# A new hand-written order of work units for attention with a maxout feed-forward layer, with fewer zero matmuls at the head and other engines for some copies

## The chip, the cores and the metric

One core of one Trainium2 chip. A core has a matmul engine (PE; its weight loads are shown apart as PEld), a vector engine (DVE), an activation engine (ACT), a third elementwise engine (POOL) and a queue engine that starts transfers (SP). The metric is the time of one execution in device microseconds, the median of several runs.

## The reference

Attention over 4 batches, 8 heads, 768 positions and 64 channels per head. A query sees the last 96 keys and the first 8 ("global") keys; distance gives a bias that falls with a slope per head. The heads are joined to 3072 rows of 512 columns, which pass through a layer with three weight matrices, of whose products the maximum is taken, and an output matrix.

```
scores = scale * q @ k.T - slope[h] * dist      # kept where global or 0 <= i - j < 96
a = exp(scores - max); a = a / (sum(a) + 1e-9)
x = (a @ v) as 3072 x 512
h = max(max(x @ w1, x @ w2), x @ w3)            # 3072 x 768
out = h @ w_out                                  # 3072 x 512
```

## The kernel before

The 3072 rows are cut into 24 tiles T of 128 rows, six to a batch. Because of the window a tile needs only its own keys and values, those of the tile before it, and the 8 global ones. The tiles are joined in seven chunks of 4, 2, 2, 4, 4, 4, 4 tiles for the feed-forward part, so its matmuls have 512 or (chunks 1 and 2) 256 columns.

The whole order of work is written by hand: SCHEDULE (lines 25 to 57) is a list of units, each a letter, numbers, and often a last number that chooses an engine. The loop at line 475 issues them one after another. Nothing is reordered later: each engine, and the SP queue too, works its own instructions off in the order of the list and waits where an operand or a buffer isn't ready. The units:

- `l n.s`, `L T`, `v T`, `w g.j`, `o i` load q and k (l in larger parts for tiles 0 to 11, L for a single tile), v, the three weights and w_out, all on the SP queue.
- `c n.s.e`, `C T.0.e`, `C T.1.e`, `W g.j.e`, `Q i.e` cast q/k, v (`C T.1`), weights and w_out to bf16. The engine e is 0 for ACT, 1 for DVE, 2 for POOL.
- `x n.s.how` and `X T.how` transpose q and k: on PE into PSUM with a copy out by ACT (0, 2), DVE (1, 3) or, in halves, both (x with 4, X with 3); `X T.4` is a transposing transfer on SP.
- `S T.g.how` makes the scores of four heads on PE (16 small matmuls for both g together; with how 1 also two matmuls that add the bias) and their exponential on ACT (line 288). `M T.g` multiplies by the mask on DVE (line 307) where how was 0.
- `G T.e` and `V T.e` put the global keys and values into the first 8 places of a tile that is no longer needed as it was.
- `A T.slot` is the product with v on PE (lines 322 and 325), then on DVE a reciprocal and a product (lines 331 and 332) into xb.
- `T T.how` transposes xb: on PE with a copy by ACT (0) or DVE (1), or (4) as a transfer on SP.
- `F c.f.j` is four matmuls of chunk c (line 361): for j=0 ACT casts the result out of PSUM (366), for j=1 and j=2 DVE takes the maximum (368, 370). `O c.t.e` is the output product, six matmuls (376), with a copy by engine e (382) and the store. `E` is the last chunk's output.
- `B h.e` and `K h` build bias and mask tables. `D i.n` issues n matmuls of zeros with 512 columns (lines 432 to 436); its first number isn't used.

Scores and products with v share two PSUM slots, sp0 and sp1, one buffer each: `A T.0` takes sp0. F, O and some transposes share three buffers called h; the other transposes share one called tp. There are six buffers for exponentials, four for h01 and three for xT.

The first feed-forward matmul, F0.0.0, needs all of tiles 0 to 3, so it comes behind A0 to A3 and T0 to T3. It is preceded on PE by the scores of tile 4.

Of the kernel before, what the change touches and what calls it, by code (L numbers as in the profile page):

```python
# [22 lines left out]


SCHEDULE = """
    K0 K1 K2 l1.0 B0.2 B1.1 B2.1 K3 K4 K5 K6 B3.0 B4.1 l1.1 D1.4 B5.0 c0.0.2 B6.0 c0.1.1 D0.4 v0 l2.0
    x0.0.3 K7 x0.1.4 c1.0.1 v1 l2.1 B7.0 S0.0.1 S0.1.1 G0.2 S1.0.0 M0.0 M0.1 c1.1.1 c2.0.2 x1.0.2 x1.1.0
    C0.1.1 A0.0 S1.1.1 G1.1 v2 v3 S2.0.1 S2.1.0 G2.1 T0.1 M1.0 M1.1 c2.1.1 S3.0.1 M2.0 M2.1 C1.1.2
    C2.1.1 M3.0 S3.1.1 M3.1 A1.0 V1.2 x2.0.2 C3.1.2 w0.0 A2.1 x2.1.0 V2.2 A3.0 T1.0 w0.1 G3.2 W0.0.2
    T2.1 T3.1 S4.0.0 S4.1.0 w0.2 F0.0.0 F0.1.0 W0.2.1 G4.2 w1.0 W0.1.2 F0.0.1 F0.1.1 F0.0.2 F0.1.2  # L30
    S5.0.0 S5.1.0 V3.2 M4.0 W1.0.2 F0.2.0 M4.1 M5.0 F0.3.0 v4 w1.1 W2.1.0 W2.0.2 F0.4.0 F0.5.0 W1.1.1
    C4.1.2 w1.2 W1.2.2 M5.1 v5 A4.1 l3.0 l3.2 l3.1 C5.1.0 V4.2 F0.2.1 c3.0.0 F0.3.1 F0.4.1 T4.0 F0.5.1
    A5.1 F0.2.2 c3.2.0 F0.3.2 W2.2.2 F0.4.2 x3.0.2 T5.1 F0.5.2 x3.2.1 F1.0.0 F1.1.0 l3.3 l4.0 F1.0.1
    F1.1.1 c3.1.2 c3.3.2 F1.0.2 x3.1.4 F1.2.0 F1.2.1 x3.3.1 F1.3.0 c4.0.0 o2 F1.1.2 o1 Q1.1 F1.4.0 Q2.2
    S6.0.0 S6.1.0 G6.2 M6.0 o0 F1.5.0 F1.2.2 F1.3.1 S7.0.0 S7.1.0 v6 l4.1 v7 F1.4.1 G7.0 M6.1 v8 F1.3.2
    x4.0.0 L12 v9 M7.0 L13 Q0.2 O0.0.1 S8.0.0 M7.1 c4.1.1 S8.1.0 C6.1.2 F1.5.1 O0.1.0 A6.0 x4.1.2 C7.1.2
    A7.1 V7.1 G8.2 F1.4.2 F1.5.2 S9.0.0 S9.1.0 G9.2 v10 T6.1 M8.0 O0.2.1 T7.1 C8.1.0 v11 S10.0.0 S10.1.0
    G10.0 M8.1 M9.0 M9.1 O0.3.0 A8.0 F2.0.0 V8.2 F2.1.0 F2.0.1 F2.1.1 C9.1.2 C12.0.2 C13.0.2 C10.1.0
    F2.0.2 F2.1.2 A9.1 M10.0 M10.1 V9.1 X12.0 F2.2.0 F2.3.0 S11.0.0 S11.1.0 T8.4 M11.0 X13.4 F2.4.0 L14
    O1.0.1 L15 T9.0 F2.2.1 A10.1 F2.5.0 V10.2 F2.3.1 F2.4.1 S12.0.0 S12.1.0 M11.1 M12.0 F2.2.2 F2.3.2  # L40
    F2.4.2 v12 C11.1.2 A11.0 C14.0.0 X14.4 T10.0 v13 v14 M12.1 v15 F2.5.1 C12.1.2 F2.5.2 O1.1.1 G12.1
    S13.0.0 S13.1.0 G13.1 T11.1 O2.0.0 F3.0.0 M13.0 F3.0.1 M13.1 F3.1.0 F3.2.0 A12.1 C15.0.0 F3.0.2
    S14.0.0 X15.4 S14.1.0 T12.4 C13.1.1 F3.1.1 F3.2.1 v16 L16 L17 G14.0 L18 A13.0 F3.1.2 F3.2.2 F3.3.0
    M14.0 T13.1 F3.3.1 F3.3.2 V13.2 S15.0.0 S15.1.0 G15.0 F3.4.0 C14.1.2 F3.5.0 M14.1 M15.0 M15.1 A14.0
    V14.2 F3.4.1 F3.5.1 T14.4 F3.4.2 C15.1.2 F3.5.2 A15.0 L19 v17 C16.0.2 C17.0.2 X16.0 O2.1.0 X17.4
    T15.1 S16.0.0 v18 v19 S16.1.0 C18.0.2 G16.0 M16.0 O3.0.1 O3.1.1 F4.0.0 V15.2 F4.1.0 F4.2.0 F4.3.0
    C16.1.2 M16.1 A16.1 C19.0.2 X18.3 X19.4 F4.0.1 F4.0.2 S17.0.0 S17.1.0 M17.0 F4.1.1 C17.1.1 F4.1.2
    S18.0.0 S18.1.0 C18.1.1 F4.2.1 F4.3.1 T16.4 M17.1 F4.2.2 F4.3.2 G18.0 S19.0.0 M18.0 M18.1 L20 M19.0
    C19.1.1 L21 S19.1.0 F4.4.0 F4.5.0 G19.2 V16.2 C20.0.0 L22 A17.0 F4.4.1 M19.1 F4.5.1 F4.4.2 F4.5.2
    X20.4 T17.4 A18.1 T18.4 A19.0 T19.4 O3.2.0 O3.3.0 C21.0.1 C22.0.0 O4.0.0 S20.0.0 S20.1.0 M20.0 X21.4  # L50
    v20 G20.0 V19.1 M20.1 O4.1.0 F5.0.0 F5.1.0 F5.2.0 F5.0.1 F5.1.1 S21.0.0 S21.1.0 F5.0.2 F5.3.0 F5.1.2
    C20.1.2 A20.1 G21.1 X22.4 V20.2 F5.4.0 L23 F5.5.0 S22.0.0 S22.1.0 v21 v22 v23 C21.1.2 C22.1.2
    C23.0.0 X23.4 M21.0 M21.1 M22.0 F5.2.1 F5.3.1 F5.4.1 F5.5.1 F5.2.2 C23.1.1 F5.3.2 A21.1 F5.4.2
    F5.5.2 G22.2 S23.0.0 T20.4 S23.1.0 T21.4 O4.2.0 M22.1 M23.0 M23.1 V21.2 A22.0 O4.3.0 V22.2 A23.1
    T22.4 T23.4 O5.0.0 O5.1.0 O5.2.0 O5.3.0 F6.0.0 F6.1.0 F6.2.0 F6.0.1 F6.1.1 F6.0.2 F6.2.1 F6.1.2
    F6.3.0 F6.2.2 F6.4.0 F6.5.0 F6.3.1 F6.4.1 F6.3.2 F6.4.2 F6.5.1 F6.5.2 E
"""


# [450 lines left out]
```

## Time and profile before

| what | value |
|---|---|
| median of 4 runs | 181.33 us (180.77 to 181.77) |
| profiled execution, its own time | 182.91 us |
| its span, first to last instruction | 181.1 us |
| PE busy | 169.4 us (94%) |
| DVE / ACT / POOL busy | 121.0 / 103.3 / 39.0 us |
| DMA read and written | 25.17 MB and 6.29 MB |

The difference of 1.8 us between the profiled time and its span lies around the instructions. PE is by far the busiest, but its share is a mean over two unlike stages: a head of some 24 us, in which the first inputs arrive, and the long rest. The rows are read stage by stage for that reason. One caution on PE: the ends of matmuls are modelled, so each row shows a duration longer than the spacing of successive matmuls; the spacing is what counts.

### The profile page before, as it was taken

The page shows a single profiled execution, that of the slowest core. Times are in us where ns is not written, and L with a number is a line of the kernel's source. Part 1 is how long each engine was busy: PE and PEld are TensorE (multiplying, and loading weights), DVE is VectorE, ACT ScalarE, POOL GpSimd, SP SyncE. Part 2 cuts the span into 40 slices and gives each one's busy share as a digit, 9 for nine tenths or more (in the row PEclk, how much of TensorE's full clock was granted, in tenths as well). Part 3 has the DMA queues.
Part 4 walks back from the last instruction along what each step waited for, and adds up shares of the span by engine and source line. Part 5 has one row for each costly group of instructions (what it writes and reads, how often), then busy time and mean ns, then how long its engine had stood idle before and what let it go on. Part 6 is the DMA issues. An engine that isn't in the chain of part 4 may idle for free.

```text
span 181.1 us, 3964 instructions
## 1 busy us (share of the span) xinstructions
PE 169.4 (94%) x1535; PEld 96.4 (53%) x1556; DVE 121.0 (67%) x236; ACT 103.3 (57%) x158; POOL 39.0 (22%) x66
## 2 busy tenths in 40 slices
PE   7688689999999999999999999999999999999991
PEld 2444544557867697744555554455445455444450
DVE  4566546788998988956988447997346995053710
ACT  5999652963597858667361765362965443513031
POOL 6313545434150061110208400100011201000000
PEclk9999969999999999999999999999999999999999
DMA  5999999999998468996999999934999624700014
GB/s 146 290 260 251 345 342 381 318 332 367 255 206 203 127 165 188 216 195 162 152 228 203 206 244 185 229 65 94 231 218 222 113 62 145 248 12 4 0 61 171
DMA packets 83586, 35.51 MB, mean 196 GB/s; under 512 B 66160, under 2 KB 78320, under 8 KB 83568
## 3 DMA queue, kind: packets, MB, share of 16 engines
q1 hardware_dynamic: 83424, 35.20, 84.4%
q8 instruction: 12, 0.20, 0.5%
q10 hardware_dynamic: 144, 0.07, 0.1%
q14 instruction: 6, 0.05, 0.1%
HBM read 25.17 MB, written 6.29 MB: 174 GB/s over the span
## 4 chain that ended last, share of the span: by engine, by line
PE 84%; SPq 5%; DMA 4%; issue 4%; POOL 1%; DVE 1%; ACT 0%; ACTq 0%; POOLq 0%
PE h L361 53%; PE po L376 16%; PE sp L283 6%; SPq L158 3%; DMA rawp<-in_k_dram 3%; PE op L322 3%; PE op L325 3%; SPq L174 2%; PE tpp L239 1%; PE xtp L349 1%; DMA out_dram<-ost 1%; PE tp L261 1%; POOL va L221 0%; DVE xb L332 0%; POOL va L189 0%
## 5 line engine op out<-in xcount | busy, mean ns | idle before, releaser
L361 PE MATMUL h<-xT,w 128*128 128x512 bf16 (+1 forms) x492 | 100.1, 350 | 0.9 <-issue 0.4
L361 PEld LDWEIGHTS <-w 128*128 128x128 bf16 x504 | 47.3, 98 | 41.5 <-issue 2.0
L288 ACT ACTIVATE P<-sp 128x1024 bf16<-128x1024 f32 (+1 forms) x48 | 43.3, 953 | 21.9 <-PE sp L283 21.6
L368 DVE TENSOR_TENSOR h<-h,h 128x512 bf16<-128x512 bf16 (+1 forms) x42 | 25.3, 609 | 20.3 <-PE h L361 19.8
L376 PE MATMUL po<-wo,ht 128*128 128x512 bf16 (+2 forms) x147 | 32.8, 362 | 0.7 <-issue 0.3
L366 ACT CAST h<-h 128x512 bf16<-128x512 f32 (+1 forms) x42 | 21.7, 533 | 20.2 <-PE h L361 19.6
L307 DVE TENSOR_TENSOR P<-P,wmask 128x1024 bf16<-128x1024 bf16 x36 | 24.2, 686 | 7.4 <-ACT P L288 7.3
L370 DVE TENSOR_TENSOR ht<-h,h 128x512 bf16<-128x512 bf16 (+1 forms) x42 | 25.2, 607 | 5.2 <-PE h L361 4.2
L376 PEld LDWEIGHTS <-ht 128*128 128x128 bf16 x156 | 14.2, 98 | 13.8
L382 ACT COPY ost<-po 128x512 f32<-128x512 f32 (+2 forms) x19 | 10.6, 561 | 18.1 <-PE po L376 15.6
L332 DVE TENSOR_TENSOR xb<-op,rz 128x512 bf16<-128x512 f32 x24 | 16.6, 691 | 0.8
L283 PEld LDWEIGHTS <-qkT 64*128 64x128 bf16 x352 | 10.3, 96 | 9.1 <-issue 7.7
L283 PE MATMUL sp<-qkT 64*128 64x128 bf16 x352 | 15.2, 223 | 0.0
L322 PEld LDWEIGHTS <-P 128*128 128x128 bf16 x192 | 12.5, 97 | 3.5 <-DVE P L307 0.5
L221 POOL COPY va<-vaf 8x260 int32<-8x260 int32 x13 | 6.2, 478 | 36.5 <-PE op L325 33.2
L322 PE MATMUL op<-va,P 128*128 128x65 bf16 x160 | 12.6, 193 | 1.3 <-POOL va L189 0.9
L189 POOL CAST va<-rawv 128x512 bf16<-128x512 f32 x12 | 7.5, 628 | 21.3 <-DMA rawv<-in_v_dram 21.1
L325 PEld LDWEIGHTS <-P 128*128 128x128 bf16 x160 | 10.5, 97 | 2.5 <-issue 1.0
L243 ACT COPY qkT<-tpp 128x1024 bf16<-128x1024 bf16 (+1 forms) x9 | 8.2, 920 | 4.6 <-PE tpp L239 4.4
L331 DVE RECIPROCAL rz<-op 128x8 f32<-128x8 f32 x24 | 4.9, 204 | 7.9 <-PE op L325 6.2
L325 PE MATMUL op<-va,P 128*128 128x65 bf16 x128 | 9.9, 193 | 0.2
L239 PE MATMUL tpp<-identb,qkp 128*128 128x128 bf16 x96 | 8.2, 234 | 1.9 <-POOL qkp L183 1.6
(69 smaller groups left out, 114.7 us busy)
## 6 DMA issues: line engine op xcount, KB each, us to landing
rawv<-in_v_dram SPq DMA_DIRECT2D x24, 256.0 KB, 5.1
out_dram<-ost SPq DMA_DIRECT2D x23, 256.0 KB, 2.3
rawp<-in_q_dram SPq DMA_DIRECT2D x6, 512.0 KB, 7.3
rawp<-in_k_dram SPq DMA_DIRECT2D x6, 512.0 KB, 7.3
wst<-in_moe_w_dram SPq DMA_DIRECT2D x3, 1024.0 KB, 10.7
raw<-in_q_dram SPq DMA_DIRECT2D x12, 256.0 KB, 4.8
raw<-in_k_dram SPq DMA_DIRECT2D x12, 256.0 KB, 4.9
wst<-in_moe_w_dram SPq DMA_DIRECT2D x3, 512.0 KB, 7.2
```

The costliest lines, as they stand in the source:

```text
L283: nc.tensor.matmul(sp[:, hh, j2, ds], qT(T - ds, 1)[hsl, jp], qT(T, 0)[hsl, jp], start=not how, stop=True, skip_group_check=True)
L288: nc.scalar.activation(P[:, :, 0:n], sp.rearrange("p a b d n -> p (a b) d n")[:, :, 0:n], AF.Exp, bias=0.0, scale=scale)
L307: nc.vector.tensor_mul(P, P, wmask[:, g, :, 0:2])
L322: nc.tensor.matmul(o, P[:, i, 0], heads(va[T])[:, h], start=True, stop=(t == 0), skip_group_check=True)
L325: nc.tensor.matmul(o, P[:, i, 1], heads(va[T - 1])[:, h], start=False, stop=True, skip_group_check=True)
L332: nc.vector.tensor_tensor(out=x.rearrange("p (g h) d -> p g h d", g=2), in0=o4[:, :, :, 0:64], in1=rz[:, :, :, None].to_broadcast([128, 2, ...
L361: nc.tensor.matmul(ps, w123[f // 2][:, dm, j, (f % 2) * 128:(f % 2) * 128 + 128], xT[c][:, dm], start=(dm == 0), stop=(dm == 3))
L366: nc.scalar.copy(h01, ps)
L368: nc.vector.tensor_max(h01s[c, f], h01s[c, f], ps)
L370: nc.vector.tensor_max(ht[c][:, f], h01s[c, f], ps)
L376: nc.tensor.matmul(po, ht[c][:, f, tt * 128:(tt + 1) * 128], wo[:, f, cols], start=(f == 0), stop=(f == NF - 1))
L382: copy(ost, po)
```

## The change

Only SCHEDULE changes. The groups of units are the same, one D block aside: before there were two (D1.4 and D0.4, eight zero matmuls), after there is one (D0.3, three). The order is new throughout, and some units have another engine. The head, up to F0.0.0, and the stage of chunks 1 and 2, from S7 to the first units of chunk 3, before and after:

```diff
-    K0 K1 K2 l1.0 B0.2 B1.1 B2.1 K3 K4 K5 K6 B3.0 B4.1 l1.1 D1.4 B5.0 c0.0.2 B6.0 c0.1.1 D0.4 v0 l2.0
-    x0.0.3 K7 x0.1.4 c1.0.1 v1 l2.1 B7.0 S0.0.1 S0.1.1 G0.2 S1.0.0 M0.0 M0.1 c1.1.1 c2.0.2 x1.0.2 x1.1.0
-    C0.1.1 A0.0 S1.1.1 G1.1 v2 v3 S2.0.1 S2.1.0 G2.1 T0.1 M1.0 M1.1 c2.1.1 S3.0.1 M2.0 M2.1 C1.1.2
-    C2.1.1 M3.0 S3.1.1 M3.1 A1.0 V1.2 x2.0.2 C3.1.2 w0.0 A2.1 x2.1.0 V2.2 A3.0 T1.0 w0.1 G3.2 W0.0.2
-    T2.1 T3.1 S4.0.0 S4.1.0 w0.2 F0.0.0 F0.1.0 W0.2.1 G4.2 w1.0 W0.1.2 F0.0.1 F0.1.1 F0.0.2 F0.1.2
...
-    S6.0.0 S6.1.0 G6.2 M6.0 o0 F1.5.0 F1.2.2 F1.3.1 S7.0.0 S7.1.0 v6 l4.1 v7 F1.4.1 G7.0 M6.1 v8 F1.3.2
-    x4.0.0 L12 v9 M7.0 L13 Q0.2 O0.0.1 S8.0.0 M7.1 c4.1.1 S8.1.0 C6.1.2 F1.5.1 O0.1.0 A6.0 x4.1.2 C7.1.2
-    A7.1 V7.1 G8.2 F1.4.2 F1.5.2 S9.0.0 S9.1.0 G9.2 v10 T6.1 M8.0 O0.2.1 T7.1 C8.1.0 v11 S10.0.0 S10.1.0
-    G10.0 M8.1 M9.0 M9.1 O0.3.0 A8.0 F2.0.0 V8.2 F2.1.0 F2.0.1 F2.1.1 C9.1.2 C12.0.2 C13.0.2 C10.1.0
...
+    K0 K1 K2 K3 K4 K5 l1.0 l1.1 D0.3 c0.0.2 B0.1 B1.1 B2.1 B3.0 K6 B4.1 B5.1 c0.1.1 c1.0.2 x0.0.4 B6.1
+    B7.1 x0.1.4 S0.0.1 v0 l2.0 l2.1 K7 S0.1.1 G0.0 S1.0.1 S1.1.0 x1.0.3 c1.1.2 M0.0 M0.1 M1.0 v1 x1.1.4
+    C0.1.2 v2 A0.1 G1.2 S2.0.1 M1.1 c2.0.2 x2.0.1 C1.1.1 S2.1.0 G2.2 S3.0.1 M2.0 M2.1 C2.1.1 T0.1 S3.1.1
+    M3.0 M3.1 c2.1.2 v3 A1.0 C3.1.0 w0.0 V1.2 x2.1.2 w1.0 A2.1 V2.2 A3.0 T1.0 T2.1 T3.1 W1.0.1 W0.0.0
+    G3.2 S4.0.0 S4.1.0 F0.0.0 F0.1.0 M4.0 F0.2.0 F0.3.0 G4.1 S5.0.0 M4.1 S5.1.0 w0.1 W0.1.1 w0.2 W0.2.2
...
+    S6.0.0 S6.1.0 v6 v7 v8 G6.0 F1.3.2 F1.5.0 v9 c4.0.1 F1.4.1 S7.0.0 S7.1.0 G7.2 v10 M6.0 M6.1 M7.0
+    M7.1 O0.0.0 F1.4.2 c4.1.1 C6.1.2 C7.1.2 L12 F1.5.1 S8.0.0 S8.1.0 x4.0.0 O0.1.0 A6.0 x4.1.2 A7.1 V7.2
+    F1.5.2 v11 T6.0 O0.2.0 T7.1 G8.2 C8.1.2 S9.0.0 S9.1.0 G9.1 v12 v13 O0.3.0 F2.0.0 F2.1.0 S10.0.0 M8.0
+    M8.1 M9.0 M9.1 S10.1.0 C9.1.2 L13 L14 F2.0.1 F2.1.1 F2.0.2 A8.0 C12.0.1 F2.1.2 G10.2 O1.0.0 V8.2
+    A9.1 X12.1 M10.0 M10.1 C10.1.0 C11.1.0 F2.2.0 S11.0.0 S11.1.0 M11.0 M11.1 L15 F2.3.0 F2.4.0 O1.1.0
+    V9.2 A10.1 F2.2.1 V10.2 T8.0 F2.3.1 F2.5.0 T9.0 A11.1 F2.4.1 T10.0 F2.2.2 F2.3.2 T11.1 F2.4.2
+    S12.0.0 S12.1.0 F2.5.1 C13.0.2 C14.0.2 C15.0.1 X13.4 F3.0.0 F3.1.0 F3.0.1 G12.1 C12.1.0 F3.2.0
...
```

The end of the list, before and after:

```diff
-    F5.5.2 G22.2 S23.0.0 T20.4 S23.1.0 T21.4 O4.2.0 M22.1 M23.0 M23.1 V21.2 A22.0 O4.3.0 V22.2 A23.1
-    T22.4 T23.4 O5.0.0 O5.1.0 O5.2.0 O5.3.0 F6.0.0 F6.1.0 F6.2.0 F6.0.1 F6.1.1 F6.0.2 F6.2.1 F6.1.2
+    T21.4 F5.4.2 F5.5.2 S23.0.0 S23.1.0 M23.0 O4.2.0 M23.1 C22.1.2 A22.0 C23.1.0 O4.3.0 V22.2 T22.4
+    A23.1 T23.4 O5.0.1 O5.1.0 O5.2.1 O5.3.0 F6.0.0 F6.1.0 F6.0.1 F6.0.2 F6.2.0 F6.3.0 F6.4.0 F6.1.1
...
```

The homes of units by engine, counted over both lists:

| unit | before ACT / DVE / POOL | after ACT / DVE / POOL |
|---|---|---|
| bias tables B | 4 / 3 / 1 | 1 / 7 / 0 |
| casts c of q, k parts | 3 / 5 / 4 | 1 / 4 / 7 |
| casts C | 8 / 8 / 20 | 12 / 7 / 17 |
| casts W of weights | 1 / 2 / 6 | 4 / 2 / 3 |
| output copies O | 14 / 6 / 0 | 15 / 5 / 0 |
| copies of T made on PE | 4 / 9 / 0 | 7 / 6 / 0 |

Of the transposes of parts, x0.0, x1.1 join x0.1 in the halved form, x3.1 leaves it, and the single copies of x1.0, x2.0, x2.1, x3.0 and x3.2 get the other engine or the other buffer. X12 goes from ACT to DVE, X16 from ACT to halves. T8 comes back from the SP queue to PE, T13 goes the other way, so eleven T and nine X stay transfers.

More of the change, by code (lines that the diff above doesn't have):

```diff
@@ L31 @@
[L31 to L34, printed above, removed]
-    S6.0.0 S6.1.0 G6.2 M6.0 o0 F1.5.0 F1.2.2 F1.3.1 S7.0.0 S7.1.0 v6 l4.1 v7 F1.4.1 G7.0 M6.1 v8 F1.3.2
@@ L36 @@
-    x4.0.0 L12 v9 M7.0 L13 Q0.2 O0.0.1 S8.0.0 M7.1 c4.1.1 S8.1.0 C6.1.2 F1.5.1 O0.1.0 A6.0 x4.1.2 C7.1.2
-    A7.1 V7.1 G8.2 F1.4.2 F1.5.2 S9.0.0 S9.1.0 G9.2 v10 T6.1 M8.0 O0.2.1 T7.1 C8.1.0 v11 S10.0.0 S10.1.0
-    G10.0 M8.1 M9.0 M9.1 O0.3.0 A8.0 F2.0.0 V8.2 F2.1.0 F2.0.1 F2.1.1 C9.1.2 C12.0.2 C13.0.2 C10.1.0
-    F2.0.2 F2.1.2 A9.1 M10.0 M10.1 V9.1 X12.0 F2.2.0 F2.3.0 S11.0.0 S11.1.0 T8.4 M11.0 X13.4 F2.4.0 L14
-    O1.0.1 L15 T9.0 F2.2.1 A10.1 F2.5.0 V10.2 F2.3.1 F2.4.1 S12.0.0 S12.1.0 M11.1 M12.0 F2.2.2 F2.3.2
@@ L41 @@
[L41 to L50, printed above, removed]
@@ L51 @@
-    v20 G20.0 V19.1 M20.1 O4.1.0 F5.0.0 F5.1.0 F5.2.0 F5.0.1 F5.1.1 S21.0.0 S21.1.0 F5.0.2 F5.3.0 F5.1.2
-    C20.1.2 A20.1 G21.1 X22.4 V20.2 F5.4.0 L23 F5.5.0 S22.0.0 S22.1.0 v21 v22 v23 C21.1.2 C22.1.2
-    C23.0.0 X23.4 M21.0 M21.1 M22.0 F5.2.1 F5.3.1 F5.4.1 F5.5.1 F5.2.2 C23.1.1 F5.3.2 A21.1 F5.4.2
-    F5.5.2 G22.2 S23.0.0 T20.4 S23.1.0 T21.4 O4.2.0 M22.1 M23.0 M23.1 V21.2 A22.0 O4.3.0 V22.2 A23.1
-    T22.4 T23.4 O5.0.0 O5.1.0 O5.2.0 O5.3.0 F6.0.0 F6.1.0 F6.2.0 F6.0.1 F6.1.1 F6.0.2 F6.2.1 F6.1.2
@@ L56 @@
-    F6.3.0 F6.2.2 F6.4.0 F6.5.0 F6.3.1 F6.4.1 F6.3.2 F6.4.2 F6.5.1 F6.5.2 E
+    K0 K1 K2 K3 K4 K5 l1.0 l1.1 D0.3 c0.0.2 B0.1 B1.1 B2.1 B3.0 K6 B4.1 B5.1 c0.1.1 c1.0.2 x0.0.4 B6.1
[3 more added lines that the diff above has]
+    G3.2 S4.0.0 S4.1.0 F0.0.0 F0.1.0 M4.0 F0.2.0 F0.3.0 G4.1 S5.0.0 M4.1 S5.1.0 w0.1 W0.1.1 w0.2 W0.2.2
@@ new lines @@
+    V3.2 F0.0.1 F0.1.1 F0.0.2 F0.1.2 v4 C4.1.0 A4.0 V4.2 w1.1 W1.1.2 W2.0.0 F0.4.0 F0.5.0 M5.0 M5.1 w1.2
+    W1.2.2 v5 W2.1.0 T4.0 F0.2.1 F0.3.1 l3.0 l3.2 F0.4.1 l3.1 c3.0.2 c3.2.2 F0.5.1 o2 C5.1.0 A5.1 l3.3
+    F0.2.2 Q2.2 F0.3.2 W2.2.0 o0 T5.0 F0.4.2 o1 F0.5.2 x3.0.0 F1.0.0 F1.1.0 c3.1.1 F1.2.0 x3.2.0 Q0.2
+    F1.0.1 F1.1.1 F1.2.1 l4.0 l4.1 c3.3.0 F1.0.2 F1.1.2 F1.2.2 x3.1.2 x3.3.1 F1.3.0 F1.4.0 Q1.2 F1.3.1
+    S6.0.0 S6.1.0 v6 v7 v8 G6.0 F1.3.2 F1.5.0 v9 c4.0.1 F1.4.1 S7.0.0 S7.1.0 G7.2 v10 M6.0 M6.1 M7.0
@@ new lines @@
+    S12.0.0 S12.1.0 F2.5.1 C13.0.2 C14.0.2 C15.0.1 X13.4 F3.0.0 F3.1.0 F3.0.1 G12.1 C12.1.0 F3.2.0
+    F3.1.1 F3.2.1 S13.0.0 S13.1.0 F2.5.2 v14 C13.1.0 C14.1.2 M12.0 M12.1 F3.0.2 F3.1.2 X14.4 F3.2.2
+    X15.4 G13.2 M13.0 M13.1 S14.0.0 S14.1.0 F3.3.0 F3.4.0 F3.5.0 M14.0 M14.1 G14.1 A12.0 A13.1 F3.3.1
+    F3.4.1 F3.5.1 S15.0.0 M15.0 S15.1.0 G15.0 v15 V13.2 L16 L17 v16 T12.4 v17 M15.1 O2.0.0 C15.1.0 A14.0
+    V14.2 F3.3.2 F3.4.2 T13.4 F3.5.2 C16.1.0 C16.0.2 X16.3 T14.4 C17.0.2 A15.1 X17.4 O2.1.0 S16.0.0
@@ new lines @@
+    S16.1.0 G16.1 L18 V15.2 L19 T15.1 M16.0 O3.0.0 M16.1 F4.0.0 F4.1.0 F4.0.1 F4.1.1 C18.0.2 L20 C19.0.2
+    A16.1 F4.2.0 F4.3.0 S17.0.0 S17.1.0 F4.2.1 F4.0.2 F4.3.1 v18 M17.0 v19 M17.1 X18.3 X19.4 C20.0.0
+    V16.2 F4.1.2 C17.1.2 O3.1.1 A17.1 F4.2.2 F4.3.2 S18.0.0 M18.0 S18.1.0 M18.1 F4.4.0 T16.4 T17.4
+    F4.4.1 C18.1.2 C19.1.1 F4.4.2 X20.4 G18.1 S19.0.0 S19.1.0 F4.5.0 L21 M19.0 M19.1 v20 F4.5.1 A18.0
+    T18.4 F4.5.2 A19.1 T19.4 V19.1 C21.0.1 X21.4 G19.1 L22 C22.0.2 L23 X22.4 O3.2.1 O3.3.0 O4.0.1
@@ new lines @@
+    S20.0.0 S20.1.0 M20.0 G20.0 O4.1.0 F5.0.0 F5.1.0 F5.2.0 S21.0.0 S21.1.0 G21.2 F5.0.1 F5.1.1 M20.1
+    M21.0 F5.3.0 F5.0.2 F5.1.2 F5.2.1 F5.2.2 v21 C20.1.1 C21.1.2 F5.4.0 S22.0.0 M21.1 S22.1.0 C23.0.0
+    F5.3.1 M22.0 M22.1 F5.5.0 F5.3.2 A20.0 V20.2 G22.2 v22 F5.4.1 X23.4 v23 F5.5.1 T20.4 A21.1 V21.1
+    T21.4 F5.4.2 F5.5.2 S23.0.0 S23.1.0 M23.0 O4.2.0 M23.1 C22.1.2 A22.0 C23.1.0 O4.3.0 V22.2 T22.4
+    A23.1 T23.4 O5.0.1 O5.1.0 O5.2.1 O5.3.0 F6.0.0 F6.1.0 F6.0.1 F6.0.2 F6.2.0 F6.3.0 F6.4.0 F6.1.1
@@ L57 @@
+    F6.2.1 F6.1.2 F6.3.1 F6.4.1 F6.2.2 F6.3.2 F6.5.0 F6.4.2 F6.5.1 F6.5.2 E
 """
```

## The prediction

> **What bounds the kernel now.** I read the page's slices first, to separate stages, then the waits of PE in the long stage, then the timeline where the long stage begins.
>
> ```profile
> span 181.1 us, 3964 instructions
> ...
> PE   7688689999999999999999999999999999999991
> ...
> PEclk9999969999999999999999999999999999999999
> ```
>
> A slice is 4.53 us. PE has room in the first six slices and is full up to the last one. The granted clock falls once, in slice six. The answer on PE's waits between 28 and 172 us is two lines:
>
> ```profile
> PE po L376 <- issue: 0.3, 2, 0.2
> PE h L361 <- issue: 0.2, 1, 0.2
> ```
>
> In 144 us PE waits half a microsecond, for nobody. All PE work stays the same there, so no other order can make this stage shorter by more than about that. A gain has to come from the head; a loss can come from anywhere. The timeline, DMA queue and PE and DVE shown alone, says what ends the head:
>
> ```profile
> 20.25 0.61 POOL L189 CAST va<-rawv 128x512 bf16<-128x512 f32 x1 [1.37 <-DMA rawv<-in_v_dram]
> ...
> 20.81 0.39 POOL L221 COPY va<-vaf 8x260 int32<-8x260 int32 x1
> ...
> 20.92 0.19 PE L322 MATMUL op<-va,P 128*128 128x65 bf16 x1 [0.93 <-POOL va L189]
> ...
> 21.26 0.19 PE L325 MATMUL op<-va,P 128*128 128x65 bf16 x1
> ...
> 22.15 0.69 DVE L332 TENSOR_TENSOR xb<-op,rz 128x512 bf16<-128x512 f32 x1
> ...
> 22.90 0.40 PE L349 MATMUL xtp<-identb,xb 128*128 128x128 bf16 x4 [0.58 <-DVE xb L332]
> ...
> 23.23 1.04 PE L283 MATMUL sp<-qkT 64*128 64x128 bf16 x16
> ...
> 24.20 0.61 PE L361 MATMUL h<-xT,w 128*128 128x512 bf16 x1
> ```
>
> v of tile 3 lands at 20.2; its cast (C3.1) lets A3 begin, its second matmul also waits for V2 (line 221), then come xb, T3, the scores of tile 4 and F0.0.0 at 24.20. The head is a chain behind the eleventh load.
>
> **The change part by part.**
>
> *Loads.* From issue plus time to landing, k of part 2 lands at 10.10 + 6.3 = 16.4, v1 at 8.39 + 6.2 = 14.6, v2 at 17.6, v3 at 20.2. After, v1 goes behind l2.1, so k2 lands some 1.2 us earlier and v1 at 16.4. The bytes ahead of v2 and v3 are the same 3.5 and 3.75 MB: both stay. A1 is the first to need v1; it began at 17.75, and 16.4 plus a DVE cast of 0.42 is 16.8, so there is cover of 0.9. DVE now waits there for v1 and for v2 (17.6), with M2.1, the copy of T0 and A1's reciprocal queued behind; A1 ends near 18.1 and needs DVE from then: nothing lost.
>
> *The chain behind v3.* C3.1 moves to ACT (0.64 against 0.63 by their rows), and V2 is no longer behind it on POOL. A3's second matmul then starts just after the first, at about 20.97 instead of 21.26: **0.3 us gained**, handed on to F0.0.0. The copy of x2.1 now stands behind C3.1 on ACT: 20.9 to 21.9, then T1 (0.60) to 22.5, then W0.0 (1.08) to 23.6. S4 and F0.0.0 need these at 22.9 and 23.9, so the gain is covered by 0.3. If W0.0 slipped by more, F0.0.0 would go back to 24.2.
>
> *Weights.* w1.0 passes w0.1 and w0.2 on SP: it lands at about 24.7 instead of 27.57, they about 2.9 later (w0.2 at 27.6 instead of 24.7). PE is given 16 matmuls with j=0 first (16 x 0.216 = 3.5 at full clock) and S5 (0.55), so F0.0.1 begins at 28.0 at the earliest, with W0.1 cast by about then. Nothing.
>
> *Zeros.* Five of eight go: they stand in a time when PE has nothing else. A rule speaks against removing them. The Trainium skill (TensorE: Matmul & The Clock Gate, section "Why this matters for your kernels") asks for 4 us of continuous work to reach the full clock. By it, the eight (spaced 0.43, 3.6 in all) almost pay for a warm PE, and three leave the next transposes and scores at half speed. The rows say that even the eight did not:
>
> ```profile
> 6.39 2.15 PE L239 MATMUL tpp<-identb,qkp 128*128 128x128 bf16 x16 [1.63 <-POOL qkp L183]
> ...
> 10.34 0.62 PE L239 MATMUL tpp<-identb,qkp 128*128 128x128 bf16 x8
> ```
>
> The 16 after the zeros take a good 1.0 per eight, against 0.62 later. By the rule the two groups and the first scores would lose about 1 us, which v3's landing would still cover; by the rows, nothing. I take nothing.
>
> *The clock's fall.* This is the largest term that can move by itself. In windows laid around the fall (the columns are the stretch, PE, PEld, DVE, ACT, POOL, then clock, DMA share, GB/s):
>
> ```profile
> 19.80:23.20 3.40, 1.74 (x32) 1.28 (x29) 1.92 (x4) 1.69 (x3) 2.14 (x4) 1.00 1.09 354
> 23.20:26.65 3.45, 3.23 (x23) 1.66 (x23) 1.63 (x2) 2.47 (x3) 1.99 (x3) 0.51 1.12 336
> ```
>
> PE is half idle for 3.4 us and then runs 3.45 us at half clock, which costs 3.45 x 0.49 = 1.7 us. The same page (section "Part 1: The HAM clock gate") has the clock drop after an idle window of about 3.4 us, in windows that do not start with the kernel. By the rule the fall can land elsewhere, or be missed, from one execution to the next; by the rows it is there. After the change the thin stretch is there too: A2 ends near 19.3, A3 waits for v3 to 20.95, and A3, T1 to T3 and part of S4 fill about 1.4 us of array time against 1.1. Ends: 1.7 gained if it goes; 0.5 lost if its whole length falls on F0. I take no difference, the row being nearest.
>
> *The long stage.* With PE always full, I compare each engine's work with PE's between the same marks, by counts times row means.
>
> From S7 to F2.0.0, after: PE has four O (24 matmuls x 0.216 = 5.2), three S (1.65), three F of 256 columns (1.3), two x (0.9), A6 and A7 (0.7), two T (0.44): 10.2. ACT has six exponentials (6 x 1.024 = 6.1), four output copies (2.4), two x copies (2.0) and T6 (0.6): 11.1. O0.0, O0.2 and T6 were DVE's. ACT is 0.9 short where before it was 0.2 short (12.5 against 12.3). Behind it stand the exponentials of S10, whose slot sp0 A8 needs. Ends: 0 and 0.9.
>
> From F2.0.0 to F3.0.0, after: PE has 17 F (7.5), S10, S11, S12 (1.4), four A (1.85), O1.0 and O1.1 (2.6), X12 (0.45), four T (0.9): 14.7. DVE has eight masks (8 x 0.686 = 5.5), six and five maxima (6 x 0.417 + 5 x 0.412 = 4.6), four pairs for A (4 x 0.895 = 3.6), C12.0 and C15.0 (1.4), X12's copy (1.2) and T11 (0.4): 16.7. DVE is 2.0 short, where before it had 2.0 to spare (14.0 against 16.0). Masks M8 and M9 now wait until after F2.0.0; C12.0 and X12 are new there. Ends: 0 and 2.0. DVE's lag may be paid in F3, whose matmuls are twice as long, and the three h buffers let it lag. Before, the stretch from 48 to 79 us already ran like this without a wait of PE:
>
> ```profile
> 48.00:63.00 15.00, 14.85 (x187) 10.21 (x187) 13.74 (x28) 12.96 (x19) 3.38 (x6) 1.00 0.82 184
> 63.00:79.00 16.00, 15.89 (x211) 12.53 (x212) 14.19 (x34) 10.61 (x19) 4.21 (x7) 1.00 0.89 186
> ```
>
> DVE and ACT at about 90% and 80% hid everything. For the two I take 0.3 each, near the lower end because that row is nearest.
>
> *Later moves.* From F3.0.0 on DVE and ACT have 4 us or more less to do than PE in each chunk. C23.1 comes to ACT behind the copy of O4.2: 149.83 + 0.63 = 150.5, and A23 began at 150.61: nothing, with 0.1 of cover. X23's transfer may go 0.5 later; it landed at 142.41 + 3.2 = 145.6 for scores at 146.97. The end (E, its stores) is unchanged.
>
> **The sum** against the profiled 182.91 (span 181.1): -0.3 + 0 + 0.3 + 0.3 = +0.3, and the same on the median: 181.33 + 0.3 = **181.6 us**. What this kernel can tell from no change is 0.5%, 0.9 us.
>
> **The rivals.**
>
> *No difference to see* (my forecast, chance 0.42): head gain and crowding cancel within 0.9 us, 180.4 to 182.2.
>
> *DVE and ACT become the bound in chunks 1 and 2* (0.35, the other side): all shortage is paid, 0.9 + 2.0 = 2.9, less 0.3: 183.9. It decides from 1.2 us of the 2.9 on. For it: the counts, and that PE has no slack to give back. Against it: the lag can be carried into F3.
>
> *The clock's fall is missed or shortened* (0.23): -1.7 - 0.3, with the crowding at 0.3: 179.6. For it: 1.4 us of array time against 1.1 in the window, and a start of F0 0.3 earlier. Against it: still under half. Here also belongs the case that the crowding costs nothing and the fall is a little shorter, 180.3.
>
> *The new order doesn't reach PE at all* is part of the first: PE's list between F0 and E holds the same matmuls.
>
> The range that leaves out two in ten cuts a tenth from each end: **179.6 to 183.5**. Faster 0.23, same 0.42, slower 0.35.
>
> **What would show it.** Right: A3's second matmul within 0.1 of its first; F0.0.0 at 23.8 to 24.0; one fall of the clock of about 3.4 us ending in F0; waits of PE between 57 and 78 us of 0.3 to 0.9 us in all, for ACT's exponentials at A8 and for DVE at A10, T9 or F2.2.1; none of note after 80. Wrong: v3 landing later than 20.6, since all of the head hangs on it; no fall or two; PE waits over 1 us in the F2 stage; or a wait in F0 for W1.0 or W0.1.

## The result, and the profile after

The changed kernel takes **180.39 us** in the median of 44 runs (180.04 to 180.71). The kernel before, in 63 runs beside it, takes 181.34 (180.45 to 183.01). The ratio is 0.9951, with a 95% interval from 0.9942 to 0.996. So the change gains 0.9 us, a small but clear gain. The forecast was a loss of 0.3, so the sign was wrong, though 180.39 lies within the range given.

The page of the changed kernel (180.36 us, the profiled execution), its span, PE's busy tenths and the granted clock:

```profile
span 178.6 us, 3963 instructions
...
PE   3598799999999999999999999999999999999991
...
PEclk9999999999999999999999999999999999999998
```

The fall of the clock that stood in slice six of the kernel before is missing. That is not the change's doing: the kernel before, profiled once more and unchanged (called b_same below), took 181.41 us with a span of 179.6, and its clock row has no fall either. Only two of its 63 runs were near 183. The execution that the prediction read, at 182.91, was one of the rare ones. From here on the changed kernel is compared with b_same.

PE's waits between 28 and 172 us in the changed kernel (total, times, longest) are one line, where there were two before:

```profile
PE h L361 <- issue: 0.2, 1, 0.2
```

None of these lines is a wait. A trace can lack some matmul records, and the place of a missing one looks like a pause. The counts of matmuls (PE) and of weight loads (PEld) tell: they agree in b_same (first line) and not in the changed kernel (second).

```profile
PE 169.5 (94%) x1556; PEld 95.8 (53%) x1556; DVE 120.9 (67%) x236; ACT 103.2 (57%) x158; POOL 38.7 (22%) x66
PE 166.8 (93%) x1529; PEld 95.6 (54%) x1551; DVE 119.0 (67%) x237; ACT 103.2 (58%) x160; POOL 37.4 (21%) x65
```

The trace that the prediction read lacks 21 matmuls. In b_same, and in a_c31pool2 (below; the changed list with one unit back on POOL; all 1551 matmuls are there), the list of waits for this stretch is empty.

The end of the changed kernel's head, in the timeline (start, duration, engine, line, operation, in brackets the idle time before it and what ended it):

```profile
20.11 0.62 ACT L189 CAST va<-rawv 128x512 bf16<-128x512 f32 x1 [0.57 <-DMA rawv<-in_v_dram]
20.27 0.39 POOL L221 COPY va<-vaf 8x260 int32<-8x260 int32 x1 [0.71 <-PE op L325]
...
20.78 0.19 PE L322 MATMUL op<-va,P 128*128 128x65 bf16 x1 [0.55 <-ACT va L189]
20.81 0.19 PE L325 MATMUL op<-va,P 128*128 128x65 bf16 x1
...
22.46 0.40 PE L349 MATMUL xtp<-identb,xb 128*128 128x128 bf16 x4 [0.58 <-DVE xb L332]
22.79 0.62 PE L283 MATMUL sp<-qkT 64*128 64x128 bf16 x16
...
23.37 0.81 PE L361 MATMUL h<-xT,w 128*128 128x512 bf16 x2
```

V2 (line 221) no longer waits for v3's cast, and A3's second matmul follows the first at once. For b_same, PE alone:

```profile
22.85 0.40 PE L349 MATMUL xtp<-identb,xb 128*128 128x128 bf16 x4 [0.58 <-DVE xb L332]
23.18 0.62 PE L283 MATMUL sp<-qkT 64*128 64x128 bf16 x16
23.85 5.34 PE L361 MATMUL h<-xT,w 128*128 128x512 bf16 x24
```

F0.0.0 begins 0.48 us earlier after the change (23.37 against 23.85). From there to the start of the last output matmul it is 151.36 us against 151.57. This 0.2 is one pause. Between the F matmuls of b_same one spacing stands out: at 50.4 us the next one begins 0.2 late. The list of waits leaves it out, because the modelled end of the matmul before covers most of it; the weight load behind it shows it:

```profile
47.98 1.56 DVE L430 CAST wo<-wost 128x1024 bf16<-128x1024 f32 x1
49.46 0.82 DVE L309 TENSOR_TENSOR P<-P,wmask 128x512 bf16<-128x512 bf16 x1
50.20 0.41 DVE L370 TENSOR_TENSOR ht<-h,h 128x256 bf16<-128x256 bf16 x1
50.67 0.31 PEld L361 LDWEIGHTS <-w 128*128 128x128 bf16 x3 [0.22 <-issue]
```

DVE casts a part of w_out (Q1), then runs a mask, and only then the maximum F1.2.2, which frees the buffer h that F1.3.2 needs. The changed list gives Q1 to POOL, a move that the table of homes leaves out, and a_c31pool2 has no such pause. Moving Q1 alone was not tried.

The remaining 0.3 lies behind the last copy of the output, in a place where no work is left. SP's waits at the end, b_same first, then the changed kernel:

```profile
SPq L505 <- DMA out_dram<-ost: 1.9, 1, 1.9
SPq L505 <- PEq L505: 0.9, 2, 0.7
```

```profile
SPq L505 <- DMA out_dram<-ost: 1.9, 1, 1.9
SPq L505 <- PEq L505: 0.6, 2, 0.4
```

Line 505 is where the program closes and its engines meet. From the end of ACT's last copy to the end of the span it is 3.0 us in b_same and 2.7 in the changed kernel. The engine that comes late is DVE. These are the drains on that line (number, then shortest, median and longest in ns, then the start of the first and of the last; the last is the one that counts), again b_same first:

```profile
L505 DVEq DRAIN  x2: 137/221/305, 175.7 to 179.3; - x2
L505 ACTq DRAIN  x2: 8/80/153, 177.0 to 178.9; - x2
```

```profile
L505 DVEq DRAIN  x2: 19/162/305, 174.9 to 178.1; - x2
L505 ACTq DRAIN  x2: 8/80/152, 176.3 to 178.1; - x2
```

DVE's last drain begins 0.4 us after ACT's in b_same, and together with it after the change.

So three places share the gain: the head 0.48, the long stage 0.2, the closing 0.3. The experiments ask what made each, and why the 0.6 us of crowding that the forecast added did not come.

### The profile page after: what moved, and what is told of

The parts are those of the page before. It is cut to its first block, busy times and chain, and to the rows that moved or that the text cites. A ratio compares the mean times of both kernels' runs of the same rounds, so it can differ in the third digit from the quotient of the medians.

```text
span 178.6 us, 3963 instructions
## 1 busy us (share of the span) xinstructions
PE 166.8 (93%) x1529; PEld 95.6 (54%) x1551; DVE 119.0 (67%) x237; ACT 103.2 (58%) x160; POOL 37.4 (21%) x65
## 4 chain that ended last, share of the span: by engine, by line
PE 83%; SPq 7%; DMA 5%; issue 1%; ACT 1%; DVE 1%; POOL 0%; ACTq 0%
PE h L361 53%; PE po L376 16%; PE sp L283 6%; SPq L158 4%; DMA rawv<-in_v_dram 4%; PE op L322 3%; SPq L174 3%; PE op L325 2%; PE tpp L239 2%; PE xtp L349 1%; DMA out_dram<-ost 1%; ACT ost L382 1%; PE tp L261 1%; DVE xb L332 0%; ACT va L189 0%
## 5 line engine op out<-in xcount | busy, mean ns | idle before, releaser
L307 DVE TENSOR_TENSOR P<-P,wmask 128x1024 bf16<-128x1024 bf16 x36 | 24.8, 716 | 3.6 <-ACT P L288 3.5
L382 ACT COPY ost<-po 128x512 f32<-128x512 f32 (+2 forms) x20 | 11.2, 564 | 18.4 <-PE po L376 11.2
L198 POOL CAST qkb<-raw 128x1024 bf16<-128x1024 f32 x7 | 7.2, 1037 | 27.6 <-DMA raw<-in_k_dram 27.5
L322 PE MATMUL op<-va,P 128*128 128x65 bf16 x160 | 12.3, 193 | 0.6 <-ACT va L189 0.5
L239 PEld LDWEIGHTS <-qkp 128*128 128x128 bf16 x96 | 6.9, 110 | 5.8 <-POOL qkp L183 4.4
```

Of the source, the lines that this page charges most:

```text
L239: nc.tensor.transpose(tp[:, e, j - lo], qb["p", n, s][:, e, 2 * j:2 * j + 2].rearrange("i h d -> i (h d)"), identb)
L307: nc.vector.tensor_mul(P, P, wmask[:, g, :, 0:2])
L322: nc.tensor.matmul(o, P[:, i, 0], heads(va[T])[:, h], start=True, stop=(t == 0), skip_group_check=True)
```

## The experiments

In the labels b_ stands for the kernel before with an edit, a_ for the changed kernel with one. Each but b_same, which is a single run, was timed beside runs of the kernel before on the same chip, whose medians lay between 181.37 and 181.49.

### The clock and the zeros

**b_fill** tried whether work in PE's idle stretches of the head changes anything by way of the clock.

```diff
-x2.1.0 V2.2 A3.0          ...  T2.1 T3.1 S4.0.0
+x2.1.0 V2.2 D0.4 A3.0     ...  T2.1 D0.3 T3.1 S4.0.0
```

> The kernel before with seven more matmuls of zeros in the thin stretch of PE before the feed-forward part: four ahead of A3 and three ahead of T3, where PE stood idle. Theory C (most of the difference is the clock: the old order leaves PE thin from A2 to T3, so in most executions the clock falls during the first feed-forward matmuls): the fall goes, 180.6 us with a narrow spread, about 0.7 under the kernel before. Theory H (the difference is the chain behind the load of v of tile 3, and the clock is chance): 181.3 as before, at most 0.2 off.

Measured: 181.29 us (180.91 to 181.49), ratio 0.9998 [0.9986, 1.0011], F0.0.0 at 23.78. Its profile has a fall of the clock from 8.9 to 12.3 us, deep in the head, and v3's landing covered that. **a_zeros8** put the zeros back:

```diff
-l1.0 l1.1 D0.3 c0.0.2
+l1.0 l1.1 D0.8 c0.0.2
```

> The changed kernel with eight zero matmuls at the head in place of three. By the prediction they stand where PE has nothing else and change nothing: 180.4. By the rule of a warm start, the transposes from 6.1 us on run at full clock more often and the head gets shorter where PE is its limit: 180.1 or less. If the early warmth brings the clock's fall back in the thin stretch: 181 and a wider spread.

Measured: 180.38 us, ratio 0.995 [0.993, 0.997], which is the changed kernel's own, with a fall of the clock from 8.0 to 11.5 us in its profile. The zeros cost and gain nothing. **b_same**, the kernel before without an edit, gave the typical profile already shown.

> The kernel before, unchanged, for a profile of an execution at its usual time: 181.3 with a span of 179.6. If the fall of the clock during the first feed-forward matmuls belongs only to the execution that was profiled first (182.9), F0.0.0 starts at 23.8 and no matmul of F0 runs at half clock; if it is usual, the fall is there again.

### The home of C3.1

**b_c31act** is the kernel before with this one home changed (`C3.1.2` to `C3.1.0`).

> The kernel before with one edit: the cast C3.1 goes from POOL to ACT, so V2 no longer waits behind it. Theory H: A3's second matmul follows the first at once, F0.0.0 is 0.3 us earlier, 181.0. Theory C: the chain is 0.3 shorter at most, but the fall of the clock stays: 181.0 to 181.3, with the spread of before.

Measured: F0.0.0 at 23.56, 0.29 earlier than in b_same, and 181.13 us (180.75 to 181.88), ratio 1.0 [0.9984, 1.0017]. In three of its twelve runs, at 181.77 to 181.88, the mean clock was 0.978. A fall over F0 would explain them, but none of the three was profiled. The ratio alone shows no gain; the profile shows 0.3 in the head.

**a_c31pool** undid it in the changed kernel (`C3.1.0` to `C3.1.2`, in place).

> The changed kernel with C3.1 back on POOL. Theory H: V2 comes behind the cast again, A3's second matmul waits 0.3 us: 180.7. Theory C: no fall of the clock in either, so the loss is the chain's alone, 180.4 to 180.7, narrow.

Measured: 185.49 us (183.52 to 186.04), ratio 1.0206 [1.0159, 1.0253]. That is a loss of 5 where 0.3 was expected, and the waits of PE in the head and F0 say why:

```profile
PE op L325 <- POOL va L221: 2.4, 2, 2.0
PE h L361 <- DVE h L368: 1.7, 1, 1.7
```

In the changed list C3.1 stands ahead of V1. On POOL V1 then waits in the queue behind a cast that waits for v3 until 20.23. A2 waits for V1, and V2 for A2, so that A2, V2 and A3 run one after another behind v3, F0.0.0 begins at 26.19, and a fall of the clock, from 21.2 to 28.0 us, reaches into F0. The second wait is another matter: a mask of tile 5 took 3.98 us, where a mask usually takes 0.69, while POOL ran four casts; the section on aligned loads comes back to this. Here a home could not be undone without its place. **a_c31pool2** undid both:

```diff
-A1.0 C3.1.0 w0.0 V1.2 x2.1.2 w1.0 A2.1
+A1.0 w0.0 V1.2 C3.1.2 x2.1.2 w1.0 A2.1
```

> The changed kernel with C3.1 back on POOL, this time behind V1 as in the old list, so that only V2 stands behind it. Theory H: A3's second matmul waits 0.3 us for V2, F0.0.0 at 23.65, 180.7. Rival (the order alone matters, the home doesn't): 180.4.

Measured: 180.73 us (180.70 to 180.83), 0.34 over the changed kernel, with F0.0.0 at 23.74. So C3.1 on ACT is worth 0.3, in both lists.

### DVE's shortage

**a_dve** gave DVE the copies of O1.0, O1.1, T8, T9 and T10, 2.6 us more in the very stage that was held to be short (`O1.0.0` to `O1.0.1`, `T8.0` to `T8.1`, and so on).

> The changed kernel with O1.0, O1.1 and the copies of T8, T9, T10 given to DVE, which adds 2 x 0.69 + 3 x 0.42 = 2.6 us to the 16.7 that DVE has between F2.0.0 and F3.0.0, where PE has 14.7. If a shortage of work time is paid (the prediction's count): about 2.6 us slower, 183.0. If what counts is only whether a result is late for its own reader, and the lag is carried into F3: at most 0.5 slower, 180.4 to 180.9.

Measured: 181.48 us (181.29 to 181.56), 1.1 over the changed kernel; F0.0.0 is unmoved at 23.39. PE's waits between 28 and 172 us:

```profile
PE xtp L349 <- DVE xT L350: 0.6, 2, 0.4
```

The changed kernel has no such line. Neither expectation held: the cost lies between 0.5 and 2.6. All 1551 matmuls are in this trace, and their starts show more than the list of waits does: pauses of 0.58 and 0.32 at 71.6 and 74.4 us, both in front of transposes whose only buffer (tp) DVE's copy has yet to free, and 0.16 at 67.0 inside scores. Together they make 1.06, and from F0.0.0 to the last output matmul it is 1.04 longer than in the changed kernel (152.40). So what was paid is mostly two copies that came late to a tile with one buffer, and the edit itself had put these copies on DVE. Whether more load alone, without such a reader, would cost anything is not shown.

### The closing, and a second cause found on the way

**b_pad8** put eight small memsets on DVE into the head of the kernel before, to see whether the number of DVE's instructions decides when it closes.

```diff
+    pad = persist.tile([128, 1], FP32, name="pad")
...
+        for _ in range(8):
+            nc.vector.memset(pad, 0.0)
```

> The kernel before with eight one-column memsets more on DVE in a gap of its head (about 0.4 us of work where DVE waits for POOL 0.9 us). Theory B (the old list's last DVE instruction comes 0.3 us late because a new block of its instructions begins just there; eight more move that point to where DVE has slack): 181.0, and the last DRAIN of DVE follows the barrier within 0.1 us. Rival (the 0.3 us at the end belongs to the output copies' new order): no change, 181.35.

Measured: 180.45 us (179.79 to 181.36), ratio 0.9957 [0.9935, 0.9979]. The closing fell to 2.7, but the gain was 1.0, and most of it lay in the head, with F0.0.0 at 22.56. The loads had become faster. The queue of SP in b_same, then in b_pad8 (line numbers there are one higher):

```profile
4.90 1.74 SPq L174 DMA_DIRECT2D rawv<-in_v_dram  x1
6.68 1.74 SPq L158 DMA_DIRECT2D rawp<-in_q_dram  x1
```

```profile
4.88 1.45 SPq L175 DMA_DIRECT2D rawv<-in_v_dram  x1
6.37 1.45 SPq L159 DMA_DIRECT2D rawp<-in_q_dram  x1
```

Of the packets between 5 and 14 us, those of 512 bytes took 34 ns in the median in b_same and 27 in b_pad8. **b_c31pad** (the same with C3.1 on ACT) and **a_pad8** (the changed kernel with the memsets and their tile) had 27 ns too:

> The kernel before with two edits: C3.1 cast on ACT, and eight one-column memsets more on DVE in the head. If the two gains found so far add (0.3 in the chain behind v3, 0.3 in the closing barrier), this is 0.6 under before, about 180.8, and what is left to the changed kernel (180.39) is 0.4 for v3's cast and the order of the long stage. If the memsets gain what their first run showed (0.97), it is about 180.2, and the changed kernel's order would have no gain of its own. In the profile of either: DVE's last drain within 0.1 us of the barrier, F0.0.0 near 23.5 with v3's cast at 20.2; if F0.0.0 is at 22.6 as in the memsets' first profile, the loads ahead of v3 will have taken 1.45 us each and not 1.74.

> The changed kernel with the same eight memsets on DVE. If they act only through the place of an instruction fetch at the end, which the changed kernel's list has moved away already, nothing changes: 180.4, closing time 2.7 us. If the memsets do something in the head (the start of the loads, or of the first bias tables), it is 0.5 or more below: 179.9 or less.

Measured: b_c31pad 180.8 us (180.18 to 181.45), ratio 0.9968 [0.9943, 0.9994]; a_pad8 180.97 (180.12 to 182.13), ratio 0.9981 [0.9954, 1.0007]. In b_c31pad the two gains did not add: on ACT v3's cast stands behind a copy of 1.01 us from 19.12 on and begins at 20.03, where on POOL in b_pad8 it began at 18.72. a_pad8 met neither of its expectations.

Another reason than the memsets was at hand. In the kernels as built the new tile takes 32 bytes of each partition, and the tiles made after it move by as much: the raw tiles (destinations of the loads) began at odd multiples of 32 and now begin at multiples of 64. Two runs parted the two causes. **b_set8** has eight memsets into a tile that was there already, so no address moves:

```diff
+        for _ in range(8):
+            nc.vector.memset(heads(va_ring[0])[:, :, 64:65], 1.0)
```

> The kernel before with eight more small memsets on DVE in the head, into a tile that is there already, so that no address moves. If the end of DVE's instructions was late in the closing barrier because of an instruction fetch, that is gone: closing time 2.7 in place of 3.0 us, DVE's last drain within 0.1 us of the barrier, packets of 512 bytes still 34 ns, F0.0.0 still near 23.85; 181.1 us. If the memsets' first gain came from the loads alone, no change: 181.4.

**b_align** moves the addresses without adding an instruction:

```diff
-    tiny = persist.tile([128, 1], FP32, name="tiny")
+    tiny = persist.tile([128, 16], FP32, name="tiny")
```

> The kernel before with the tile tiny 16 columns wide, which moves every later tile by 32 bytes and adds no instruction. If addresses set the loads' pace: packets of 512 bytes in 27 ns, one load of 512 KB every 1.45 us, v3 landing near 18.7 and F0.0.0 near 22.6, closing time still 3.0 us; 180.7 us, spread over a microsecond by falls of the clock. If it was the memsets: 34 ns and 181.4.

Measured: b_set8 181.18 us (180.53 to 181.43), ratio 0.999 [0.9975, 1.0005], packets 34 ns, closing 2.7. SP's wait at the end has the changed kernel's form (lines are two higher):

```profile
SPq L507 <- PEq L507: 0.6, 2, 0.4
```

b_align: 180.65 us (180.11 to 181.43), ratio 0.9968 [0.9945, 0.9992], packets 27 ns, F0.0.0 at 22.99, closing 3.0 as in b_same. Both expectations held, but for v3's cast in b_align, which began at 19.15, with F0.0.0 0.4 later than expected. Eight more instructions on DVE alone take the 0.3 out of the closing in the profile; the times (0.2 by the medians, with an interval that includes no change) fit but don't prove it. The addresses alone are worth 0.6 to 0.7. The changed kernel left the addresses as they were (34 ns), so this second cause is no part of its gain.

### Aligned loads in the changed kernel, and the second floor

In the changed kernel the faster loads cost time. a_pad8, timeline around 32 us:

```profile
31.77 2.02 POOL L428 CAST w<-wst 128x1024 bf16<-128x1024 f32 x2
...
32.32 4.44 DVE L308 TENSOR_TENSOR P<-P,wmask 128x1024 bf16<-128x1024 bf16 x2
...
33.74 2.48 POOL L184 CAST qkp<-rawp 128x1024 bf16<-128x1024 f32 x2
...
36.69 2.55 DVE L369 TENSOR_TENSOR h<-h,h 128x512 bf16<-128x512 bf16 x4
```

Two masks, usually 0.69 us each, take 4.44 together (the longer one 3.0), while POOL runs four casts without a gap because their loads have all landed. PE then waits 1.6 us for the maxima behind the masks. In the changed kernel itself, where these casts come one by one, the same masks take 1.03 and 0.68. The Trainium skill (SBUF — State Buffer, section "Who interferes with whom") has this: an instruction of DVE with two inputs from SBUF contends with one of POOL that reads SBUF, and one of the two is held. The trace agrees, and here it was mostly DVE's: only the last of the four casts was longer too, 1.42 us in place of 1.03. **a_align** repeats it without memsets, **a_alignfix** also moves the two masks:

```diff
-F0.0.1 F0.1.1 F0.0.2 F0.1.2 ... F0.5.0 M5.0 M5.1 w1.2 ... T4.0 F0.2.1 F0.3.1
+F0.0.1 F0.1.1 M5.0 F0.0.2 M5.1 F0.1.2 ... F0.5.0 w1.2 ... F0.2.1 T4.0 F0.3.1
```

> The changed kernel with tiny 16 columns wide. If the addresses and not the memsets did it: as with the memsets and their tile, packets of 27 ns, F0.0.0 near 23.1, a wait of PE of about 1.6 us near 36 behind the masks of tile 5, 180.9 us. If the memsets did it: 180.4 without the wait.

> As the last, with the two masks of tile 5 (M5) moved ahead on DVE, out of the reach of the four casts on POOL, and T4 one unit later. If the masks were held up by the casts, they take 0.7 us each again, PE's wait near 36 is gone or under 0.5, and the time is 179.3 to 179.7, under both kernels. If the wait was for something else, it stays and the time is 180.9.

Measured: a_align 180.96 us (179.85 to 182.15), ratio 0.9992 [0.9963, 1.0021], with the longer mask at 2.0 us and PE's wait at 0.6, not 1.6, in its profile; a_alignfix 180.2 (179.97 to 180.38), ratio 0.9938 [0.9919, 0.9956]. The masks in the latter, alone on DVE:

```profile
29.95 0.68 DVE L307 TENSOR_TENSOR P<-P,wmask 128x1024 bf16<-128x1024 bf16 x1
...
31.15 0.69 DVE L307 TENSOR_TENSOR P<-P,wmask 128x1024 bf16<-128x1024 bf16 x1
```

The wait is gone and the spread with it, but 179.3 to 179.7 was missed. **a_v1** had already hinted at why. It loads v1 ahead of the second half of part 2, as before:

```diff
-v0 l2.0 l2.1 ... M1.0 v1 x1.1.4
+v0 l2.0 v1 l2.1 ... M1.0 x1.1.4
```

> The changed kernel with the load of v1 back ahead of the second half of part 2 of q and k, as before. If the order of these two loads costs and gains nothing, as the prediction had it, 180.4. If k2's landing 1.2 us earlier is what lets the head of the changed kernel run ahead of v3, A1 and the scores of tiles 2 and 3 start later and A3 with them: 180.8 or more. If that order is what keeps the changed kernel's times so close together, its times will spread over 1 us as those of before do.

Measured: 180.44 us (180.23 to 180.75), no difference. In its profile, whether by this order or by chance, v3 could be cast from 19.01 on, and PE went ahead only for a while:

```profile
22.91 1.89 PE L361 MATMUL h<-xT,w 128*128 128x512 bf16 x7
25.07 1.90 PE L361 MATMUL h<-xT,w 128*128 128x512 bf16 x8 [0.28 <-DVE w L427]
26.91 0.62 PE L283 MATMUL sp<-qkT 64*128 64x128 bf16 x16
```

F0.0.0 is 0.46 us earlier than in the changed kernel's profile, but F0.2.0 waits for the cast W1.0, and S5 begins at 26.91 in both. That cast waited for its load, w1.0, up to 24.32. Close behind v3's chain stands a second floor, the weights: their landing, then their casts. **a_alignfix2** moved the mask M4.1 on DVE behind the cast W0.1, which was late in a_alignfix, where M4.1 took 1.49 us beside a cast on POOL; **a_same** is the changed kernel once more.

```diff
-S5.0.0 M4.1 S5.1.0 w0.1 W0.1.1
+S5.0.0 S5.1.0 w0.1 W0.1.1 M4.1
```

> As a_alignfix, with M4.1 on DVE moved behind the cast W0.1. If that cast is the floor, F0.0.1 begins near 26.9 in place of 27.34 and PE keeps the lead: 179.8 to 179.9. If another cast or load stands right behind it, 180.2 as a_alignfix.

> The changed kernel as it is: 180.4, packets of 34 ns, F0.0.0 near 23.4, closing time 2.7 us.

Measured: a_alignfix2 180.3 us (180.07 to 180.39), a_same 180.36 (180.24 to 180.65). F0.0.1 began at 27.20, not 26.9, and PE's weight loads wait 0.5 us for a cast on POOL. The next weight stands right behind. No version beat the changed kernel by more than the 0.1 to 0.2 us between these medians.

## Why the prediction was wrong, step by step

The forecast was -0.3 in the head, +0.6 of crowding and nothing else, so +0.3. Measured in the profiles: -0.48, 0, then -0.2 in the long stage and -0.3 at the end.

- **The base.** The sum was made against 182.91, an execution with 3.45 us at half clock, and carried to the median unchanged. "I take no difference" for the clock's fall gave the right term for the median, but by luck: b_same has no fall over F0 to keep or lose. The times gave a hint: the profiled one lay 1.58 above the median, about what the fall was worked out to cost (1.7). A fall somewhere is common, though: 64 of 124 runs of the kernel before, beside the experiments, had a mean clock of 0.99 or less, and 58 of these took 181.8 us or less. F0.0.0 began at 23.85 in a typical run, not 24.20, so "23.8 to 24.0" after the change was really no gain.
- **The chain behind v3: right.** 0.3 was forecast; 0.29 (b_c31act) and 0.34 (a_c31pool2) were measured. A3's second matmul came 0.03 after the first. A further 0.1 to 0.2 came with v3's cast, which began at 20.11 against 20.20, and with the chain behind it.
- **Loads: right** (a_v1: 180.44). **Zeros: right** (a_zeros8: 180.38); the rule that spoke against it costs nothing here because v3's landing covers that part of the head.
- **Weights: right in the cost, and without cover.** The cast of W1.0 began at 24.29 in a_same, as soon as its load had landed, and F0.2.0 took its weights at once. This floor costs nothing at F0.0.0 = 23.37 and caps further gains in the head.
- **The long stage, "for the two I take 0.3 each": the step that failed.** The counts of work may stand, but the price was 0. Between 28 and 172 us PE has no wait for ACT or DVE in the changed kernel, and a_c31pool2, with no record missing, has none either. A shortage counted between two marks is not a delay as long as buffers let the engine lag and the next stage gives it time. The prediction's own row of a stretch with DVE at 90% pointed this way, though it wasn't quite "without a wait": the 0.2 at 50.4 us, for DVE, lies in it. a_dve shows where the reserve ends, at a late copy out of a single buffer. ACT's part was not tried by itself.
- **"The end is unchanged": the second failure.** The closing became 0.3 shorter. No unit of the list is there; eight more instructions on DVE ahead of it were enough in the old list (b_set8). That the new list acts in the same way was not tried apart.
- **"In 144 us PE waits half a microsecond, for nobody": a wrong reading.** Those pauses are missing matmul records. They appear in each trace that lacks 21 or 22 matmuls and in none that has them all, of either list, and with them (b_fill, b_c31act) or without (b_same) the stage takes 151.56 or 151.57. The real slack was the 0.2 at 50.4 us, and the changed list gained it.
- **Later moves: right**, no wait after 80 us.

With the terms measured, 0.48 in the head (0.3 of it C3.1's home), 0.2 in the long stage and 0.3 in the closing make 0.98; the two profiled spans differ by 1.0 and the medians by 0.95. Of the rivals, the one with DVE and ACT as the bound fell with the list of waits. The one of a missed fall came nearest in time, with its side case that "the crowding costs nothing", but the clock had no part in it: neither of the two profiles compared has a fall.

## What to carry to other kernels

Before a sum is carried from a profile to a median, compare their times: a profile 0.9% above its median holds an event that typical runs don't have. A shortage of an engine off the critical path is priced by the waits that comparable stretches show, and that can be zero; only an experiment tells how far the reserve reaches. Before waits are read, compare the counts of matmuls and weight loads: missing records look like waits, and real waits can hide behind modelled ends, so look at the spacing of starts. A gain in a chain is worth at most the distance to the next chain behind it, so ask for the second floor before counting on the first.

## What the runs showed of the hardware

- **Where a load's destination begins in SBUF matters.** With raw tiles at odd multiples of 32 bytes a 512-byte packet took 34 ns, at multiples of 64 it took 27, in every kernel of either kind. Only these two placements were tried, and other tiles moved with the raw ones, so the exact rule is open. The page's line of the main queue (packets, MB, share of 16 engines' span), for b_same and then for b_pad8, says the same of the whole run:

```profile
q1 hardware_dynamic: 83424, 35.20, 85.2%
```

```profile
q1 hardware_dynamic: 83424, 35.20, 75.8%
```

- **DVE and POOL can hold each other up**: a mask of 0.69 us took 1.03 beside one cast on POOL (the changed kernel), 3.0 and 3.98 beside casts that followed each other without a gap (a_pad8, a_c31pool). Faster loads brought the two together.
- **The end of the program can depend on how many instructions an engine has had.** Eight more on DVE took the closing from 3.0 to 2.7 us. In the five profiles with the late drain an 8 KB fetch of instructions is recorded at the very end (179.93 us in b_same); in the others the last such fetch comes earlier (170.85 in b_set8). But in b_same it starts 0.5 us after the late drain has ended, so it isn't what the drain waited for. The cause stays open.
- **A fall of the clock cost nothing where PE wasn't the bound**: from 8.9 to 12.3 us F0.0.0 kept its place (b_fill, 23.78). From 23.2 to 26.6 us, over S4 and F0, the span was 1.5 us longer (181.1 in the first profile against 179.6 in b_same).
- **Two groups of times.** About a quarter of the runs of the kernel before lay at 180.45 to 180.86, the rest mostly at 181.2 to 181.8, while the changed kernel's lay within 0.7 us. An earlier landing of v3 in some executions, which the second floor caps in the changed kernel, would explain both; a_v1's profile shows the cap, but no profile of the faster group was caught.
